# Moving the steps of a float64 weight conversion inside a matmul stage: new distances, split stores, later first loads

## The chip, the cores and the metric

The program runs on one core of a Trainium2 chip. The metric is the device time of one execution in microseconds (us), lower is better. The engines are named as in the profile: PE (matrix products), ACT (ScalarE), DVE (VectorE), POOL (GpSimd) and SP, which here issues every DMA, one after the other from one queue.

## The reference, cut to what matters

Three layers stand behind each other: a chunked state-space scan, a mixture of four experts over 3072 tokens, and a gated layer whose weights come in as float64.

```python
# x: scan output, (3072, 256)
for e in range(4):
    h = np.maximum(x @ w1[e], 0.0)                    # w1[e]: 256 x 1024
    out += p[:, e:e + 1] * (h @ w2[e])
...
g = x @ w_gate                                        # w_gate, w_val: 256 x 1536, float64
silu = g * (1.0 / (1.0 + np.exp(-g)))
val = x @ w_val
return (silu * val @ w_out).astype(np.float32)        # w_out: 1536 x 256, float64
```

## The kernel before, in words

Every product is formed three times, from a high and a low part of each operand (`high` rounds on ACT, L602; `low` subtracts the high part from the value, mostly on POOL, L605). The program has three stages.

First come the **units**: experts 0 and 1 on part of the tokens, mixed with the scan. Then come the **blocks**, the stage that the change is in: eight pairs (expert, pair of token blocks), `blocks` in the code, each cut in four **quads** (two 128-wide slices of the hidden layer). The text writes quad 3.1 for block 3, quad 1. Last come the **dense** quads of the float64 layer, 18 of them.

A quad of the block stage has four **parts** (0 to 3), the stretches between the `yield`s of `expert_hidden`. PE runs 45 matmuls of 512 columns in it: 21 for seven products (L829) and 24 that project the quad before (L928). Four accumulators X, Y, Z, W take the products, and other engines move them along:

- in part 0, ACT copies X into Y (L884), and PE may then add to Y;
- in part 1, ACT copies Y into Z (L887) and W aside (L889); in part 2 it copies Z aside (L892);
- in part 2, DVE adds that copy to W (L895) and the other to Y (L899). ACT rounds the four results (`hh`, L878) and DVE forms their low parts (`hl`, L879). The last `hl`, of key 12, is read from Z in part 3.

PE can't write X in the next quad before the `hl` of key 11 has read it, nor can ACT overwrite Y (L884 of the next quad) before the `hl` of key 21 has.

After each block, in quad 0 (parts 2 and 3) of the next one, DVE and POOL add the projected block to `acc` (L939, L940).

Between the parts stand side jobs. A table `todo` has a list of steps for each slot (block and quad, part), and they are emitted behind that part's own instructions, so each engine runs them in that order. The side jobs are

- `expert_quad`: the weights of the next expert. It loads a quad (L625, L626), rounds it on ACT, forms four sums on DVE (L612 to L615, 128x128 each, here called the expert sums) and low parts on POOL;
- `dense_tokens` and `expert_tokens`: sums and high and low parts of the tokens;
- `dense_quad`: the conversion of float64 weights, for g in 0..5 and for gate, val and out (0g, 0v, 0o, 1g, ... in the text). `load` fetches 512 KB as 32-bit words; `s0` (ACT, L678, L679) and `s1` (DVE, L683 to L685) build the float32 words, `s2` (DVE, L690) adds the last bit and, for gate and val, forms four sums on POOL; `s3` (ACT) and `s4` (POOL) form high and low parts of the first columns, `s5` and `s6` those of the sums, and `store` writes both to DRAM (L718, L721);
- `dense_load`: reads converted weights back (L733, L736), five DMAs for a dense quad. The first two, `dense_load(0, 0)` and `dense_load(0, 1)`, are side jobs of the block stage.

Tiles come from pools with rings of buffers. A tile that takes a used buffer waits until the last reader of the old tile is done, on the engine that writes the new one. `hh` and `hl` have five buffers each (`HB`), `f64` two, `dr` two, and the high and low tiles of the conversion (`wd_h`, `wd_l`) one each. `wd_o`, the tile of the output weights, takes the buffer of `wd_h`. Expert weights and re-read dense weights share 16 buffers (`wpool`).

The conversion's slots come from fixed offsets: with a the slot of the load, the steps of gate and val stand at a + 0, 3, 4, 5, 7, 8, 8, 9, 10, and the next conversion begins 6 slots later.

Of the kernel before, what the change touches and what calls it, by code (L numbers as in the profile page):

```python
# [23 lines left out]
def kernel(ctx: ExitStack, tc: tile.TileContext, nat_d, bc_d, bc0_d, a_d, probs, w1, w2, wg, wv, wo, out):  # L24
# [537 lines left out]
    def m_hidden(u):  # L562
        e, t, f = u
        o, n, vh, vl, _ = place(u)
        if f == FC1 // 2:
            pbc[e, t] = mpool.tile([P, 512], F32, tag="ma", name="pbc")[:, :n]
            nc.sync.dma_start(out=pbc[e, t], in_=probs_d[e:e + 1, o:o + n].to_broadcast([P, n]))
        ph = hidden_bank(n)
        hidden(ph, W1[e, f // NG], f % NG, vh, vl)
        hh = hpool.tile([P, 512], F32R, tag="hh", name="hh")[:, :n]  # L570
        hl = hpool.tile([P, 512], F32R, tag="hl", name="hl")[:, :n]
        nc.scalar.activation(out=hh, in_=ph, func=AF.Relu)  # L572
        nc.vector.scalar_tensor_tensor(out=hl, in0=ph, scalar=0.0, in1=hh.bitcast(F32), op0=ALU.max, op1=ALU.subtract)  # L573
        hid[u] = hh, hl
# [77 lines left out]

    HIGH = np_f32(0x0FEFFFFF)

    def dense_quad(g, what):

        V = nc.vector  # L660
        r = {}

        def load():
            f = r["f"] = raw_p.tile([P, 2, FQ, 2], I32, tag="raw", name="f64")
            if what == 2:
                src = wo[g * FQ:(g + 1) * FQ, :].rearrange("(k p) d -> p k d", p=P)
            else:
                src = (wg, wv)[what][:, g * FQ:(g + 1) * FQ].rearrange("(k p) f -> p k f", p=P)
            nc.sync.dma_start(out=f.rearrange("p k n w -> p k (n w)"), in_=src.bitcast(I32))
            f = f.rearrange("p k n w -> p (k n) w")  # L670
            r["hi"] = f[:, :, 1]
            r["lo"] = f[:, :, 0]
            r["byte"] = f.bitcast(U8)[:, :, 3]

        def s0():
            m = r["m"] = dpools["cv"].tile([P, 2 * FQ], I32, tag="wr", name="dr", bufs=2)
            m = m.bitcast(F32)
            nc.scalar.activation(out=m, in_=r["hi"].bitcast(F32), func=AF.Abs, scale=2.0**-112)  # L678
            nc.scalar.activation(out=r["lo"], in_=r["byte"], func=AF.Copy, scale=1 / 32, bias=1 / 64)  # L679

        def s1():
            m = r["m"].bitcast(F32)
            V.tensor_scalar(out=m, in0=m, scalar1=HIGH, scalar2=None, op0=ALU.min)  # L683
            V.tensor_scalar(out=r["m"], in0=r["m"], scalar1=3, scalar2=None, op0=ALU.logical_shift_left)
            V.scalar_tensor_tensor(  # L685
                out=r["m"], in0=r["hi"], scalar=-0x80000000, in1=r["m"], op0=ALU.bitwise_and, op1=ALU.bitwise_or
            )

        def s2():
            V.tensor_tensor(out=r["m"], in0=r["m"], in1=r["lo"], op=ALU.add)  # L690
            r["m"] = r["m"].bitcast(F32)
            if what < 2:
                r["s"] = r["f"].rearrange("p k n w -> p (k n w)").bitcast(F32)[:, :2 * FQ]
                gate_sums(r["m"], r["s"], nc.gpsimd)

        def s3():
            if what < 2:
                r["out"] = [dpools["cv"].tile([P, W7], F32R, tag=f"w{z}", name=f"wd_{z}") for z in "hl"]
                high(r["out"][0][:, RAW], r["m"][:, P:])
            else:  # L700
                r["out"] = [dpools["cv"].tile([P, 2, 2 * DM], F32R, tag="wh", name="wd_o")]
                high(r["out"][0][:, 0, :], r["m"])

        def s4():
            if what < 2:
                low(r["out"][1][:, RAW], r["m"][:, P:], r["out"][0][:, RAW])
            else:
                low(r["out"][0][:, 1, :], r["m"], r["out"][0][:, 0, :])

        def s5():  # L710
            high(r["out"][0][:, SUM], r["s"])

        def s6():
            low(r["out"][1][:, SUM], r["s"], r["out"][0][:, SUM])

        def store():
            if what == 2:
                nc.sync.dma_start(out=wo_d[g], in_=r["out"][0].bitcast(F32))  # L718
                return
            for z, v in enumerate(r["out"]):  # L720
# [144 lines left out]
    def expert_hidden(e, p, j):  # L865


        X, Y, Z, W = (bank(*b) for b in banks[:4])
        w = WE[e, j][0]
        V, S = nc.vector, nc.scalar  # L870
        part3, v = temp("c1"), temp("c1")
        add = lambda ps, a, x, start=False: product(ps, w, a, operand(p, x), start)

        def out(key, ps):
            hh = hpool.tile([P, 512], F32R, tag="hh", name="hh")
            hl = hpool.tile([P, 512], F32R, tag="hl", name="hl")
            hid[e, p, j, key] = hh, hl
            S.activation(out=hh, in_=ps, func=AF.Relu)  # L878
            return lambda: V.scalar_tensor_tensor(  # L879
                out=hl, in0=ps, scalar=0.0, in1=hh.bitcast(F32), op0=ALU.max, op1=ALU.subtract  # L880
            )

        add(X, A11, "B11", True)
        S.activation(out=Y, in_=X, func=AF.Copy)  # L884
        yield
        add(Y, S2, "T2")
        S.activation(out=Z, in_=Y, func=AF.Copy)  # L887
        add(W, S3, "T3", True)
# [58 lines left out]
    def dense_hidden(p, q, what, s):  # L947

        w = wq.pop((p, q, what))
        V = nc.vector  # L950

        def out(key, ps, add, dst):

            if what == 0:
                s[key] = temp("s")
                if add is not None:
                    V.tensor_tensor(out=s[key], in0=ps, in1=add, op=ALU.add)  # L957
                nc.scalar.activation(out=s[key], in_=ps if add is None else s[key], func=AF.Silu)  # L958
                return
            if add is not None:  # L960
                V.tensor_tensor(out=dst, in0=ps, in1=add, op=ALU.add)  # L961
            av = s.pop(key)
            V.tensor_tensor(out=av, in0=ps if add is None else dst, in1=av, op=ALU.mult)  # L963
            ah = hpool.tile([P, 512], F32R, tag="hh", name="ah")
            al = hpool.tile([P, 512], F32R, tag="hl", name="al")
            nc.scalar.activation(out=ah, in_=av, func=AF.Copy)  # L966
            low = V if (p, q) == quads[-1] and key in (12, 21) else nc.gpsimd
            low.tensor_tensor(out=al, in0=av, in1=ah.bitcast(F32), op=ALU.subtract)  # L968
            hid[p, q, key] = ah, al

        return seven(p, w, out)
# [33 lines left out]
    with tc.manual_schedule():  # L1005
        nc.sync.dma_start(out=la, in_=a_d)
        expert_load(0, 0)
        for q in range(NFIRST):
            a_load(q)
            a_load_nat(q)  # L1010
            Q[q]["L"] = [hpool.tile([P, 4, P], F32, tag=("hh", "hl")[q], name="L") for _ in range(2)]
        nc.sync.dma_start(out=pin, in_=probs)
        a_load(2)
        expert_load(0, 1)
# [54 lines left out]

        def job(steps, at):  # L1070
            for fn, a in zip(steps, at, strict=True):
                put(a + (a >= n0 and (a - n0) % 4 == 2 and fn.__name__ in ("s1", "s2", "sums")), fn)

        for j, a in enumerate((138, 146, 154, 161)):
            job(expert_quad(2, j), [a + o for o in (0, 4, 5, 7, 8, 9, 10)])
# [22 lines left out]
        a = quad(0, 1)  # L1098
        for g in range(NQD):
            for what in range(3):  # L1100
                while any((a + o - n0) % (4 * NQE) in (2, 3, 4) for o in (4, 5)):
                    a += 1
                job(dense_quad(g, what), [a + o for o in ((0, 3, 4, 5, 7, 8, 8, 9, 10) if what < 2 else (0, 3, 4, 5, 7, 8, 9))])
                a += 6 if what < 2 else 5
        assert a <= quad(7, 2)
        spread(dense_tokens(0), quad(6, 1), quad(7, 2))
        put(quad(6, 3, 2), lambda: dense_load(0, 0))
        put(quad(7, 1, 2), lambda: dense_load(0, 1))

        def at(*key):  # L1110
            for fn in todo.pop(key, []):
# [112 lines left out]
```

## Time and profile before

| what | value |
|---|---|
| time, median of 3 runs | 861.83 us (860.66 to 862.84) |
| the profiled execution, its own time | 863.37 us |
| its span, first to last instruction | 861.6 us |
| PE busy | 838.8 us (97%) |
| ACT, DVE, POOL busy | 462.3, 609.7, 442.7 us |
| mean granted clock of PE | 0.993 |

The profiled execution stands 1.54 us above the median of the runs. PE is idle for 22.8 us of the span; a busy PE can still be slow, since its matmuls overlap and its clock can be halved, so the length of a quad says more than its busy time.

### The profile page before, as it was taken

What the parts mean: (1) busy time and instruction counts of PE and PEld (TensorE: products, weight loads), DVE (VectorE), ACT (ScalarE), POOL (GpSimd) and SP (SyncE); (2) the same over time, 40 slices, a digit from 0 to 9 for tenths busy, and PEclk for the clock granted to TensorE, in tenths of its full rate; (3) what the DMA queues carried; (4) which work ended last, traced back from release to release, by engine and by line L of the source; (5) the groups of instructions that cost most, each with busy time, mean ns of one, the idle gap of its engine ahead of it and who ended that gap; (6) DMA issues with size and microseconds to landing.
All of it is one profiled execution on the core that took longest, in us unless ns stands there. A gap on an engine that the chain in (4) does not pass through costs nothing. (4 is left out here: it accounts for less than half of the span.)

```text
span 861.6 us, 12496 instructions
## 1 busy us (share of the span) xinstructions
PE 838.8 (97%) x4394; PEld 692.8 (80%) x4394; DVE 609.7 (71%) x895; ACT 462.3 (54%) x824; POOL 442.7 (51%) x389
## 2 busy tenths in 40 slices
PE   8899999999999999999999999899999999999998
PEld 7898778888878888878887878687888888888886
DVE  5987889767756756697977566547676667666665
ACT  6655555555476666667665566444444544434443
POOL 5865776445586622546664254307463664534251
PEclk9999999999999999999999999899999999999999
DMA  7854454435321235344532222653454274537301
GB/s 214 296 174 136 142 179 150 150 129 191 97 77 68 90 105 179 113 126 135 169 104 64 110 81 104 213 171 129 153 177 153 92 268 137 170 112 266 111 1 50
DMA packets 53623, 120.33 MB, mean 140 GB/s; under 512 B 5496, under 2 KB 19512, under 8 KB 53560
## 3 DMA queue, kind: packets, MB, share of 16 engines
q1 hardware_dynamic: 53560, 119.52, 41.4%
q8 instruction: 35, 0.57, 0.3%
q14 instruction: 28, 0.23, 0.1%
HBM read 102.06 MB, written 17.45 MB: 139 GB/s over the span
## 5 line engine op out<-in xcount | busy, mean ns | idle before, releaser
L968 POOL TENSOR_TENSOR al<-s,ah 128x512 fp32r<-128x512 f32 x70 | 103.4, 1507 | 126.0 <-issue 91.1
L966 ACT ACTIVATE ah<-s 128x512 fp32r<-128x512 f32 x72 | 45.3, 632 | 101.3 <-DVE s L963 85.4
L895 DVE TENSOR_TENSOR d<-d,c 128x512 f32<-128x512 f32 x32 | 22.3, 698 | 85.2 <-ACT c L892 85.1
L928 PE MATMUL d<-hh,we_o 128*128 128x512 f32 x256 | 79.8, 393 | 0.0
L928 PE MATMUL po<-hh,we_o 128*128 128x512 f32 x256 | 79.0, 390 | 0.5 <-DVE acc L594 0.5
L879 DVE SCALAR_TENSOR_TENSOR hl<-h,hh 128x512 fp32r<-128x512 f32 x96 | 66.1, 689 | 18.2 <-ACT hh L878 14.2
L572 ACT ACTIVATE hh<-h 128x512 fp32r<-128x512 f32 (+1 forms) x80 | 40.5, 510 | 67.5 <-PE h L531 67.5
L878 ACT ACTIVATE hh<-h 128x512 fp32r<-128x512 f32 x96 | 57.3, 597 | 27.9 <-DVE h L899 23.1
L573 DVE SCALAR_TENSOR_TENSOR hl<-h,hh 128x512 fp32r<-128x512 f32 (+1 forms) x80 | 45.9, 577 | 34.7 <-ACT hh L572 34.3
L845 DVE TENSOR_TENSOR u<-h,c 128x512 f32<-128x512 f32 x36 | 24.9, 690 | 56.8 <-PE h L829 37.9
L531 PE MATMUL h<-xh,w_h 128*128 128x512 f32 (+1 forms) x160 | 57.4, 359 | 4.3 <-DVE hl L573 3.4
L605 POOL TENSOR_TENSOR we_l<-raw_q,we_h 128x384 fp32r<-128x384 f32 (+1 forms) x32 | 37.8, 1180 | 45.0 <-ACT we_h L602 45.0
L539 PE MATMUL po<-hh,w_h 128*128 128x512 f32 (+1 forms) x160 | 57.4, 359 | 1.9 <-DVE acc L588 1.2
L829 PE MATMUL h<-xh,wq_h 128*128 128x512 f32 x144 | 56.8, 394 | 1.7 <-DVE v L847 1.1
L958 ACT ACTIVATE s<-s 128x512 f32<-128x512 f32 x54 | 33.4, 629 | 44.1 <-DVE s L957 43.4
L928 PEld LDWEIGHTS d<-hh,we_o 128*128 128x128 f32 x256 | 48.6, 190 | 10.3
L928 PEld LDWEIGHTS po<-hh,we_o 128*128 128x128 f32 x256 | 48.0, 188 | 10.9 <-ACT we_o L602 0.9
L531 PE MATMUL h<-xh,w_l 128*128 128x512 f32 (+1 forms) x160 | 56.1, 350 | 0.2 <-POOL w_l L143 0.2
L829 PE MATMUL h<-xh,wq_l 128*128 128x512 f32 x144 | 56.1, 390 | 0.0
L829 PE MATMUL h<-xl,wq_h 128*128 128x512 f32 x144 | 56.1, 389 | 0.0
L531 PE MATMUL h<-xl,w_h 128*128 128x512 f32 (+1 forms) x160 | 56.1, 350 | 0.0
L539 PE MATMUL po<-hh,w_l 128*128 128x512 f32 (+1 forms) x160 | 56.0, 350 | 0.0
(226 smaller groups left out, 2494.4 us busy)
## 6 DMA issues: line engine op xcount, KB each, us to landing
wq_h<-wd_d SPq DMA_DIRECT2D x36, 448.0 KB
wq_l<-wd_d SPq DMA_DIRECT2D x36, 448.0 KB
bc<-in_bc_dram SPq DMA_DIRECT2D x22, 512.0 KB
L<-crow_d SPq DMA_DIRECT2D x22, 512.0 KB
wq_o<-wo_d SPq DMA_DIRECT2D x18, 512.0 KB
raw_q<-in_w_dram SPq DMA_DIRECT2D x32, 256.0 KB
nat<-in_nat_dram SPq DMA_DIRECT2D x24, 256.0 KB
pbc<-probs_d SPq DMA_DIRECT2D x22, 256.0 KB
```

Of the source, the lines that this page charges most:

```text
L531: nc.tensor.matmul(ps, w[:, k, fs], v[:, k, :], start=(i == 0), stop=(i == len(ops) - 1))
L539: nc.tensor.matmul(po[d], w[:, fc, dsl], x, start=(first and i == 0), stop=(last and i == 2))
L572: nc.scalar.activation(out=hh, in_=ph, func=AF.Relu)
L573: nc.vector.scalar_tensor_tensor(out=hl, in0=ph, scalar=0.0, in1=hh.bitcast(F32), op0=ALU.max, op1=ALU.subtract)
L605: engine.tensor_tensor(out=out, in0=raw, in1=hi.bitcast(F32), op=ALU.subtract)
L829: nc.tensor.matmul(ps, x[:, ws], y, start=(start and i == 0), stop=(i == 2), skip_group_check=True)
L878: S.activation(out=hh, in_=ps, func=AF.Relu)
L879: return lambda: V.scalar_tensor_tensor(out=hl, in0=ps, scalar=0.0, in1=hh.bitcast(F32), op0=ALU.max, op1=ALU.subtract)
L928: nc.tensor.matmul(po[d], both[:, z, dsl], y, start=(first and i == 0), stop=(last and i == 2), skip_group_check=True)
L958: nc.scalar.activation(out=s[key], in_=ps if add is None else s[key], func=AF.Silu)
L966: nc.scalar.activation(out=ah, in_=av, func=AF.Copy)
L968: low.tensor_tensor(out=al, in0=av, in1=ah.bitcast(F32), op=ALU.subtract)
```

## The change

The conversion's steps get distances from the step before (`gap`) and a set of allowed parts of a quad: a step whose slot falls on another part moves on to the next that is allowed. `EARLY` is parts 0 and 1 (for `s0`), `SUMS` parts 0, 1 and 3, without part 3 of a block's quad 0 and part 0 of its quad 1 (for `s1` and `s2`), `CALM` parts 0 to 2 (for `s3` and `s5`). The store is split: the high part goes out one slot after `s5`, and the low part one slot after `s6`. `wd_o` gets a buffer of its own (`wo`). The ring of `hl` (with `al` and one use in the scan) gets four buffers where it had five. The first two dense loads move from quads 6.3 and 7.1 to quads 7.1 (part 3) and 7.3, and `dense_tokens(0)` begins two parts later.

```diff
-        hl = hpool.tile([P, 512], F32R, tag="hl", name="hl")[:, :n]
+        hl = hpool.tile([P, 512], F32R, tag="hl", name="hl", bufs=LAG + 1)[:, :n]
...
+    ANY, EARLY, SUMS, CALM = (0, 1, 2, 3), (0, 1), (0, 1, 3), (0, 1, 2)
...
-                r["out"] = [dpools["cv"].tile([P, 2, 2 * DM], F32R, tag="wh", name="wd_o")]
+                r["out"] = [dpools["cv"].tile([P, 2, 2 * DM], F32R, tag="wo", name="wd_o")]
...
-        def store():
-            if what == 2:
+        def store(z=None):
+            if z is None:
                 nc.sync.dma_start(out=wo_d[g], in_=r["out"][0].bitcast(F32))
-                return
-            for z, v in enumerate(r["out"]):
-                nc.sync.dma_start(out=wd_d[g, what, :, z, :], in_=v.bitcast(F32))
-
-        return [load, s0, s1, s2, s3, s4] + ([s5, s6] if what < 2 else []) + [store]
+            else:
+                nc.sync.dma_start(out=wd_d[g, what, :, z, :], in_=r["out"][z].bitcast(F32))
+
+        late = [(s5, 0, CALM), (lambda: store(0), 1, ANY), (s6, 0, ANY), (lambda: store(1), 1, ANY)]
+        return [(load, 0, ANY), (s0, 3, EARLY), (s1, 2, SUMS), (s2, 1, SUMS), (s3, 2, CALM), (s4, 1, ANY)] + (
+            late if what < 2 else [(store, 1, ANY)]
+        )
...
-                while any((a + o - n0) % (4 * NQE) in (2, 3, 4) for o in (4, 5)):
-                    a += 1
-                job(dense_quad(g, what), [a + o for o in ((0, 3, 4, 5, 7, 8, 8, 9, 10) if what < 2 else (0, 3, 4, 5, 7, 8, 9))])
-                a += 6 if what < 2 else 5
-        assert a <= quad(7, 2)
-        spread(dense_tokens(0), quad(6, 1), quad(7, 2))
-        put(quad(6, 3, 2), lambda: dense_load(0, 0))
-        put(quad(7, 1, 2), lambda: dense_load(0, 1))
+                at = a
+                for fn, gap, parts in dense_quad(g, what):
+                    at += gap
+                    while (at - n0) % 4 not in parts or parts is SUMS and (at - n0) % (4 * NQE) in (3, 4):
+                        at += 1
+                    put(at, fn)
+                a += 7 if what < 2 else 5
+        spread(dense_tokens(0), quad(6, 1, 3), quad(7, 2))
+        put(quad(7, 1, 3), lambda: dense_load(0, 0))
+        put(quad(7, 3), lambda: dense_load(0, 1))
```

The moved steps can be read in the order of three engines. Line numbers of the change are up to 5 higher for the same code.

**SP, from the load of 5v on (quad 6.3 before, quad 6.2 in the change).** `wq` is a dense load, `wd_d<-wd_h` and `wd_d<-wd_l` the stores of 5g and 5v, `f64` a load of the conversion, `pbc` the expert shares. Before:

```order
L669 DMA f64_5539<-in_wv_dram 128x2x512
L733 DMA wq_h_5593<-wd_d_102 128x896
L733 DMA wq_l_5594<-wd_d_102 128x896
L733 DMA wq_h_5597<-wd_d_102 128x896
L733 DMA wq_l_5598<-wd_d_102 128x896
L736 DMA wq_o_5601<-wo_d_103 128x1024
L721 DMA wd_d_102<-wd_h_5555 128x896
L721 DMA wd_d_102<-wd_l_5556 128x896
```

The same stretch in the change:

```order
L672 DMA f64_5498<-in_wv_dram 128x2x512
L721 DMA wo_d_103<-wd_o_5464 128x1024
L723 DMA wd_d_102<-wd_h_5587 128x896
L672 DMA f64_5650<-in_wo_dram 128x2x512
L723 DMA wd_d_102<-wd_l_5588 128x896
L950 DMA pbc_5749<-probs_d_100 128x512
L950 DMA pbc_5751<-probs_d_100 128x512
L723 DMA wd_d_102<-wd_h_5685 128x896
L723 DMA wd_d_102<-wd_l_5686 128x896
L738 DMA wq_h_5803<-wd_d_102 128x896
```

The five DMAs of the first dense load stood ahead of all the stores of 5g and 5v, and stand behind them now.

**DVE, quads 3.1 and 4.1, from the addition of the finished block to the sum of W.** `raw_q` has the expert sums, `dr` is `s1`. Quad 3.1 before:

```order
L939 TENSOR_TENSOR pbc_3791<-d2_3778,pbc_3791 128x512
L612 TENSOR_TENSOR raw_q_3990<-raw_q_3990 128x128
L613 TENSOR_TENSOR raw_q_3990<-raw_q_3990 128x128
L614 TENSOR_TENSOR raw_q_3990<-raw_q_3990 128x128
L615 TENSOR_TENSOR raw_q_3990<-raw_q_3990 128x128
L683 TENSOR_SCALAR dr_4173<-dr_4173 128x512
L684 TENSOR_SCALAR dr_4173<-dr_4173 128x512
L685 SCALAR_TENSOR_TENSOR dr_4173<-f64_4090,dr_4173 128x512
L895 TENSOR_TENSOR d0_4150<-d0_4150,c1_4152 128x512
```

In the change quad 3.1 has no `s1` at this place (its `s1` stands behind the quad's last `hl`), and quad 4.1, which had none, reads:

```order
L944 TENSOR_TENSOR pbc_4195<-d2_4182,pbc_4195 128x512
L612 TENSOR_TENSOR raw_q_4393<-raw_q_4393 128x128
L613 TENSOR_TENSOR raw_q_4393<-raw_q_4393 128x128
L614 TENSOR_TENSOR raw_q_4393<-raw_q_4393 128x128
L615 TENSOR_TENSOR raw_q_4393<-raw_q_4393 128x128
L686 TENSOR_SCALAR dr_4476<-dr_4476 128x512
L687 TENSOR_SCALAR dr_4476<-dr_4476 128x512
L688 SCALAR_TENSOR_TENSOR dr_4476<-f64_4398,dr_4476 128x512
L900 TENSOR_TENSOR d0_4558<-d0_4558,c1_4560 128x512
```

So the pattern of sums and `s1` ahead of W's addition leaves quad 3.1 and comes up in quad 4.1; quad 5.1 has it in both.

**ACT, from the rounding of key 21 in quad 6.3 to the copies of quad 7.0.** `dr` and `f64<-f64` are `s0` of 5v, `wd_h` is `s3` or `s5` of 5g, `t3h` and `xh1` are tokens. Before:

```order
L878 ACTIVATE hh_5578<-h1_5524 128x512
L602 ACTIVATE wd_h_5555<-f64_5414 128x512
L602 ACTIVATE t3h_0_98<-acc1_91 128x512
L602 ACTIVATE xh1_79<-acc1_91 128x512
L878 ACTIVATE hh_5607<-h2_5525 128x512
L678 ACTIVATE dr_5618<-f64_5539 128x512
L679 ACTIVATE f64_5539<-f64_5539 128x512
L884 ACTIVATE h1_5622<-h0_5621 128x512
L887 ACTIVATE h2_5623<-h1_5622 128x512
```

In the change:

```order
L883 ACTIVATE hh_5578<-h1_5519 128x512
L602 ACTIVATE wd_h_5587<-dr_5447 128x384
L883 ACTIVATE hh_5594<-h2_5520 128x512
L602 ACTIVATE t3h_0_98<-acc1_91 128x512
L602 ACTIVATE xh1_79<-acc1_91 128x512
L889 ACTIVATE h1_5613<-h0_5612 128x512
L602 ACTIVATE wd_h_5587<-f64_5336 128x512
L892 ACTIVATE h2_5614<-h1_5613 128x512
```

Five side instructions stood between the rounding of key 21 and the copy of X; now there are three, none of them `s0`.

## Rows read from the trace of the kernel before

**Rows 1.** Waits of PE (waited for: total us, times, longest):

```profile
PE h L829 <- ACT h L884: 6.0, 7, 3.1
```

**Rows 2.** Windows: stretch, length, busy time (count) of each engine, PEclk, DMA share, GB/s:

```profile
558.20:568.40 10.20, 10.20 (x47) 8.45 (x45) 6.10 (x11) 5.27 (x9) 1.29 (x1) 1.00 0.45 138
278.53:370.35 91.82, 91.82 (x406) 75.97 (x405) 63.05 (x102) 59.04 (x106) 37.76 (x40) 1.00 0.36 121
370.35:393.36 23.01, 21.00 (x92) 16.74 (x90) 19.09 (x29) 14.15 (x27) 14.47 (x15) 1.00 0.35 115
414.33:435.04 20.71, 20.70 (x91) 16.81 (x90) 18.42 (x29) 14.73 (x28) 15.44 (x16) 1.00 0.45 145
456.00:478.22 22.22, 21.06 (x91) 16.73 (x90) 16.76 (x25) 13.38 (x25) 11.70 (x12) 1.00 0.28 90
498.62:510.57 11.95, 10.50 (x46) 8.37 (x45) 9.82 (x15) 7.36 (x13) 7.77 (x5) 1.00 0.29 89
530.97:541.72 10.75, 10.50 (x46) 8.37 (x45) 7.80 (x12) 7.61 (x14) 5.74 (x7) 1.00 0.08 5
541.72:558.20 16.48, 13.35 (x47) 10.42 (x45) 7.41 (x12) 6.87 (x12) 7.14 (x5) 0.79 0.67 237
546.30:553.10 6.80, 6.05 (x14) 4.79 (x15) 0.00 (x0) 3.57 (x7) 5.03 (x4) 0.50 0.65 230
```

**Rows 3.** Timeline of SP around quads 6.3 to 7.1 (start, length):

```profile
516.69 0.61 SPq L733 DMA_DIRECT2D wq_l<-wd_d  x1
540.33 0.32 SPq L736 DMA_DIRECT2D wq_o<-wo_d  x1
540.75 0.38 SPq L721 DMA_DIRECT2D wd_d<-wd_h  x1
```

**Rows 4.** Timeline of ACT, same stretch (in brackets: idle before, and whom it waited for):

```profile
532.20 0.68 ACT L679 ACTIVATE f<-f 128x512 int32<-128x512 uint8 x1
532.76 0.61 ACT L884 ACTIVATE h<-h 128x512 f32<-128x512 f32 x1
...
545.99 0.52 ACT L602 ACTIVATE wd_h<-dr 128x384 fp32r<-128x384 f32 x1 [4.77 <-DMA wd_d<-wd_h]
546.42 0.58 ACT L884 ACTIVATE h<-h 128x512 f32<-128x512 f32 x1
```

**Rows 5.** Timeline of PE, quad 7.1:

```profile
547.05 0.80 PE L829 MATMUL h<-t24h,we_h 128*128 128x512 f32 x1 [3.13 <-ACT h L884]
```

**Rows 6.** Timeline of DVE, quad 3.1 (from 370.35):

```profile
373.96 0.28 DVE L612 TENSOR_TENSOR raw_q<-raw_q 128x128 f32<-128x128 f32 x1
374.27 1.29 DVE L613 TENSOR_TENSOR raw_q<-raw_q 128x128 f32<-128x128 f32 x1
...
378.07 1.24 DVE L683 TENSOR_SCALAR dr<-dr 128x512 f32<-128x512 f32 x1
...
380.41 0.69 DVE L895 TENSOR_TENSOR d<-d,c 128x512 f32<-128x512 f32 x1
```

**Rows 7.** Timeline of POOL, quad 3.1, its last operation in that run of work:

```profile
377.96 1.06 POOL L605 TENSOR_TENSOR we_l<-raw_q,we_h 128x384 fp32r<-128x384 f32 x1
```

**Rows 8.** Timeline of DVE, quad 4.1 (from 414.33):

```profile
422.11 0.68 DVE L895 TENSOR_TENSOR d<-d,c 128x512 f32<-128x512 f32 x1
```

**Rows 9.** Timeline of POOL, quad 4.1:

```profile
420.70 1.34 POOL L605 TENSOR_TENSOR we_o<-raw_q,we_o 128x512 fp32r<-128x512 f32 x1
```

**Rows 10.** Timeline of ACT, quad 6.1 (from 498.62):

```profile
503.82 0.63 ACT L602 ACTIVATE xh<-acc 128x512 fp32r<-128x512 f32 x1 [1.58 <-POOL acc L940]
504.36 0.58 ACT L887 ACTIVATE h<-h 128x512 f32<-128x512 f32 x1
```

**Rows 11.** Timeline of DVE, quad 7.2 (from 558.20), sum of W and the last two `hl`:

```profile
564.47 0.70 DVE L895 TENSOR_TENSOR d<-d,c 128x512 f32<-128x512 f32 x1 [3.80 <-ACT c L892]
...
567.17 1.45 DVE L879 SCALAR_TENSOR_TENSOR hl<-h,hh 128x512 fp32r<-128x512 f32 x2
```

**Rows 12.** Timeline of ACT, quad 7.3 (from 568.40):

```profile
571.32 0.58 ACT L887 ACTIVATE h<-h 128x512 f32<-128x512 f32 x1 [1.46 <-PE h L829]
```

More of the change, by code (lines that the diff above doesn't have):

```diff
@@ L875, in out @@
             hh = hpool.tile([P, 512], F32R, tag="hh", name="hh")
-            hl = hpool.tile([P, 512], F32R, tag="hl", name="hl")
+            hl = hpool.tile([P, 512], F32R, tag="hl", name="hl", bufs=LAG + 1)
             hid[e, p, j, key] = hh, hl
@@ L964, in out @@
             ah = hpool.tile([P, 512], F32R, tag="hh", name="ah")
-            al = hpool.tile([P, 512], F32R, tag="hl", name="al")
+            al = hpool.tile([P, 512], F32R, tag="hl", name="al", bufs=LAG + 1)
             nc.scalar.activation(out=ah, in_=av, func=AF.Copy)
@@ L1010 @@
             a_load_nat(q)
-            Q[q]["L"] = [hpool.tile([P, 4, P], F32, tag=("hh", "hl")[q], name="L") for _ in range(2)]
+            Q[q]["L"] = [hpool.tile([P, 4, P], F32, tag=("hh", "hl")[q], name="L", bufs=(HB, LAG + 1)[q]) for _ in range(2)]
         nc.sync.dma_start(out=pin, in_=probs)
@@ L1071, in job @@
             for fn, a in zip(steps, at, strict=True):
-                put(a + (a >= n0 and (a - n0) % 4 == 2 and fn.__name__ in ("s1", "s2", "sums")), fn)
+                put(a + (a >= n0 and (a - n0) % 4 == 2 and fn.__name__ == "sums"), fn)
         for j, a in enumerate((138, 146, 154, 161)):
```

## The prediction

> **What bounds the kernel now.** The table has PE busy for 97% of the span, so I first asked what a quad of the block stage takes when nothing holds it, and then which quads take longer. The windows answer both. Quad 7.2 takes 10.20 us, and the nine quads from 1.0 to 3.0 take 91.82 together, which is 9 x 10.20 [rows 2]. That is 45 matmuls at 0.227 us, PE's pace at full clock. Every us that a quad takes beyond 10.20 is therefore a stall, and a step that moves inside that cover is worth nothing.
>
> The other windows show the stalls [rows 2]: quads 3.1 and 3.2 together 23.01 - 20.40 = 2.61; quad 7.0 10.75 - 10.20 = 0.55 (three such: 4.0, 4.3 and 7.0); 4.1 and 4.2 together 0.31; 5.1 and 5.2 together 1.82; 6.1 1.75; 7.1 6.28. The sum is 2.61 + 3 x 0.55 + 0.31 + 1.82 + 1.75 + 6.28 = 14.42 us. The waits of PE say through whom most of it comes: the copy of X into Y on ACT, 6.0 us in 7 waits, one of 3.1 [rows 1]. The timelines then tell what stood ahead of that copy in each place.
>
> **Quad 7.1 (6.28 us): a store behind a blocked queue.** SP issued a dense load at 516.69 and its next DMA, the output weights' load, at 540.33: nearly 24 us, two quads and more. The store of 5g's high part, next in line, left at 540.75 [rows 3]. ACT's `s3` of 5v needs that tile, waited 4.77 us for the store and ran at 545.99, and the copy of X behind it ran at 546.42 [rows 4]. PE stood for 3.13 us [rows 5], and then its granted clock was 0.50 for 6.80 us (1.2 GHz instead of 2.4) [rows 2]; half of those 6.80 us, 3.4, is lost work, and 3.13 + 3.4 is about the 6.28.
> In the change the dense load stands behind both stores of 5v, so the output weights' tile, which needs a buffer that an expert's weights hold, keeps no store back. The store of 5g's high part now stands one slot behind `s5`, and `s3` of 5v one slot after that. That is short, so I checked the times: `s5` runs before the copy of Y, which starts 2.92 into a clean quad (571.32 - 568.40) [rows 12], and a store took 5.2 us from issue to the start of the instruction that it held (540.75 to 545.99) [rows 3, 4]. It lands 8.2 into quad 7.0 at the latest; `s3` stands behind the rounding of key 21, whose low part starts at 567.17 - 558.20 = 8.97 [rows 11]. So `s3` doesn't wait, if SP is free. I take the whole 6.28 as removed.
> The first dense quad begins two quads (20.4 us) after 7.1. If its five DMAs (2.3 MB) are issued at the end of 7.1 and move at the 237 GB/s of the busiest window [rows 2], they need 10 us. The next five are issued in 7.3 and are wanted a dense quad (66 matmuls, 15 us) after the first begins. I cost both at nothing; a load that came late would cost its lateness, one for one.
>
> **`s0` at the end of a quad (3 x 0.55).** In 6.3 `s0` stands between part 3's rounding and the copy of X in 7.0. Its second instruction starts at 532.20 and the copy at 532.76, 1.79 after quad 7.0 began (530.97) [rows 4, 2]; in a clean quad the copy would start 0.88 after (571.32 less a product and a projection, 9 matmuls or 2.04, less 568.40) [rows 12]. `EARLY` puts every `s0` into parts 0 and 1, where it has 2.04 us between the two copies and the wait of PE behind them. Removed: 1.65. The work that stays in parts 2 and 3 (two roundings of expert weights and one of the conversion, or three of tokens in 6.1) is three instructions where five made 0.55 of stall; two fewer, 0.56 apart [rows 4], take 1.1 off, so I cost it at nothing.
>
> **Token step in 6.1 (1.75).** The copy of Y started at 504.36, 5.74 into the quad, behind a rounding of tokens that waited for POOL's addition to `acc` and ran at 503.82 [rows 10]. That addition belongs to quad 6.0's last parts and is done 5.2 into 6.1. The step now stands in part 3, after 8 us, and finds its input there. Removed: 1.75.
>
> **`s1` behind the expert sums (3.1 before, 4.1 in the change, 5.1 in both).** After a block, DVE adds three pieces to `acc`, then the expert sums run: 0.28 for the first and 1.29 for the second, though they have one shape; the four took 378.07 - 373.96 = 4.11 in 3.1 while POOL worked [rows 6]. `s1` came next, 2.34 us (378.07 to 380.41), and W's sum started 10.06 into the quad instead of 6.27 [rows 6, 11]: 3.79 late, for 2.61 us of stall. Quad 4.1 had the sums without `s1`: W's sum started at 422.11 - 414.33 = 7.78, 1.51 late, for 0.31 [rows 8, 2]. So a delay costs about itself less 1.2.
> - In 3.1 `s1` goes behind the last `hl`, and the quad becomes what 4.1 was: 2.61 - 0.31 = 2.30 removed.
> - In 4.1 `s1` comes in. The bounds: 5.1, which has the same pattern, cost 1.82 [rows 2]; at the upper end, POOL works longer here. Its run ended at 377.96 + 1.06 = 379.02 in 3.1 [rows 7], just as the first instruction of `s1` ended; in 4.1 it has one 128x512 low part more (`s4` of 2o), 1.34 by its neighbour [rows 9], so the other two may be slowed too and `s1` may take 2.34 + 1.3 = 3.6, which gives 1.51 + 3.6 - 1.2 = 3.9. I take 3.0, between them and nearer 3.1's 2.61. Added: 3.0 - 0.31 = 2.7.
> - In 5.1 only the owner of `s1` changes (3o for 4g): nothing.
>
> The Trainium skill (SBUF — State Buffer, section Who interferes with whom) has the ports that DVE and POOL share as an exclusive lock: a DVE instruction with two SBUF inputs or in a two-port mode waits for the whole POOL instruction. The 1.29 beside 0.28 [rows 6] agrees. By that rule all three instructions of `s1` in 4.1 would wait for a POOL instruction each, which is the second rival.
>
> **The rings.** With four `hl` buffers the low part of key 12 can't start before PE has projected the same key of the quad before, which ends with the quad. In 7.2 it started 0.76 after 567.17, at 567.93 [rows 11], and the quad ended at 568.40: the wait is 0.5 us. Z, which it reads, is overwritten by the copy of Y at 571.32 [rows 12], 2.2 us after the delayed low part is done, and DVE's next fixed task is W's sum, 6.27 into the quad. Cost: nothing. If that cover were gone, see the third rival. The loads of the conversion now often wait on SP until the conversion before has freed its buffer, and loads of expert weights queue behind them; `s0` then has a part less of reserve in 2.3, and DVE has `s1`, sums and `s2` between quads 2.3 and 3.0. Neither shows in the trace of before. Lower bound nothing, upper bound one small stall of each kind (0.56 + 0.56); I take 0.4.
>
> **The sum.** Removed 6.28 + 1.65 + 1.75 + 2.30 = 12.0; added 2.7 + 0.4 = 3.1; net 8.9. The profiled execution took 863.37 and would take 854.5. It stood 1.54 above the median of the runs, 861.83, from which the same 8.9 give **852.9**.
>
> **Rivals.**
> 1. *The sums meet no stall.* If `s1` in 4.1 and 5.1 falls into pauses of POOL, the 2.7 is nearer 0 and part of 5.1's 1.82 goes too: 848.5 to 850.5. Against it: the sums took over 4 us there each time. 0.12.
> 2. *DVE is held longer.* If each of the three instructions of `s1` in 4.1 waits for one of POOL (1.34 [rows 9]), `s1` takes 4.0, the stall 1.51 + 4.0 - 1.2 = 4.3 and the sum 1.3 more: 854.2. The same in 2.3, 3.0 and 4.2, where `s1` stands just ahead of sums, adds up to as much in each: 854.5 to 858.5 together. For it: 4.1's POOL run is the longest. 0.16.
> 3. *Slower: the ring of four.* If the low part of key 12 were held past the next quad's copy of Y, more than 2.2 us beyond what I worked out, each of 31 quads would end late by the wait of 0.5: 15 us, 868. Against it: PE's order puts that projection at the quad's end, not later. 0.05.
> 4. *The stall at the end isn't gone.* `s3` of 5v still waits for the store, if SP is held at that moment by a DMA that waits for POOL; the margin is 0.7 us. PE would stand and its clock fall again, up to 6.28 back: 859.2, no change that can be told. 0.07.
>
> **How the numbers follow.** The forecast (850.5 to 854.5) has 0.60, and the rivals the rest. The range 848.5 to 858.5 takes in the forecast and the first two and leaves out the last two. 0.3% (2.6 us) is about what a measurement of this kernel can tell from no change: faster than 859.2 are the forecast, rivals 1 and 2, 0.88; rival 4 is the same, 0.07; rival 3 is slower, 0.05.
>
> **What would show it.** Right: quads 7.0 and 7.1 at 10.2, no fall of the granted clock between them, no gap of SP over some 10 us ahead of the last stores; 4.3, 6.1 and 4.0 at 10.2; 3.1 and 3.2 together about 20.7; 4.1 and 4.2 together about 23.4. Wrong: a wait of PE over 1 us in another quad of blocks 2 to 4 (ACT behind a load, or DVE behind `s1`), a wait for dense weights at the start of the dense stage, or a last `hl` that holds the copy of Y.

## The result, and the profile after the change

The changed kernel takes 855.04 us (median of 4 runs, 854.79 to 855.87) and the kernel before 862.34 (4 runs): a ratio of 0.9916, 95% interval 0.9893 to 0.9939. It is 7.3 us faster; 8.9 were predicted, 852.9 us, in a range of 848.5 to 858.5. The profiled execution has a span of 853.2 us (861.6 before). The 852.9 was counted from 861.83, the median of before at that time; with its fourth run that median is 862.34, so 0.5 of the 2.1 us between forecast and result lies in the base.

From the first matmul of quad 0.0 to that of the first dense quad the changed kernel takes 333.53 us, the kernel before 340.72. So 7.19 us were saved in the block stage. The units ahead of it took 1.12 less, which is inside their spread: over the 13 traces of this study their length goes from 236.0 to 238.8 us. The dense stage behind it took 282.92 us (283.05 before), so the two later dense loads cost nothing there, as the prediction had it.

The waits of PE on the copy of X have shrunk from 6.0 us to 1.8, as [rows 1] show it for before; a wait for DVE is new (waited for: total us, times, longest):

```profile
PE h L834 <- DVE hl L884: 2.2, 2, 2.0
...
PE h L834 <- ACT h L889: 1.8, 3, 1.0
```

The windows after (columns as in [rows 2]) are those of quad 3.0; 3.1 and 3.2 together; 4.1 and 4.2; a piece of 4.2; 5.1 and 5.2; and, behind the cut, 7.0 and 7.1:

```profile
359.37:370.57 11.20, 10.48 (x46) 8.37 (x45) 9.56 (x17) 7.90 (x16) 6.69 (x8) 1.00 0.45 142
370.57:391.21 20.64, 20.64 (x92) 16.74 (x90) 18.72 (x30) 14.19 (x28) 14.32 (x15) 1.00 0.47 147
411.61:435.91 24.30, 22.28 (x92) 17.98 (x90) 20.13 (x29) 14.10 (x27) 14.66 (x15) 0.93 0.33 108
423.94:427.36 3.42, 3.37 (x8) 2.70 (x9) 2.45 (x4) 2.76 (x7) 1.28 (x1) 0.50 0.97 315
456.31:478.50 22.19, 21.01 (x92) 16.74 (x91) 19.72 (x29) 12.56 (x23) 11.50 (x12) 1.00 0.21 72
...
529.49:549.89 20.40, 20.40 (x91) 16.90 (x90) 15.11 (x22) 13.64 (x25) 14.40 (x14) 1.00 0.44 145
```

Set against 10.20 a quad they give the stalls, in us (single quads by their first matmuls):

| quads | before | predicted | after |
|---|---|---|---|
| 7.1 | 6.28 | 0 | 0 |
| 4.0, 4.3, 7.0 | 1.65 | 0 | 0 |
| 6.1 | 1.75 | 0 | 0.01 |
| 3.1 + 3.2 | 2.61 | 0.31 | 0.24 |
| 4.1 + 4.2 | 0.31 | 3.0 | 3.90 |
| 5.1 + 5.2 | 1.82 | 1.82 | 1.79 |
| 1.2, 2.3, 3.0 (small delays) | 0.02 | 0.4 | 1.37 |

The removed part came as forecast. Both added terms were larger: 4.1 by 0.9 and the small delays by 1.0.

**What happens at 7.0 and 7.1.** SP and ACT after (start, length; in brackets the idle time before and its releaser):

```profile
531.52 0.32 SPq L723 DMA_DIRECT2D wd_d<-wd_h  x1
...
547.01 0.32 SPq L723 DMA_DIRECT2D wd_d<-wd_l  x1
547.38 0.47 SPq L738 DMA_DIRECT2D wq_h<-wd_d  x1
```

```profile
538.33 0.52 ACT L602 ACTIVATE wd_h<-dr 128x384 fp32r<-128x384 f32 x1
```

The store of 5g's high part leaves at 531.52, `s3` of 5v runs at 538.33 without a wait, and the dense load comes behind all four stores. Before, the same store left at 540.75 and `s3` waited 4.77 us [rows 3, 4]. SP still issues nothing for 14.4 us ahead of that store (its DMA before is at 516.83). But here the store waits for its own data: `s5` of 5g ends at 531.49, and both quads take 10.20.

**What happens in 4.1.** DVE (from the second of the expert sums, the next two cut), POOL and PE after:

```profile
415.53 1.29 DVE L613 TENSOR_TENSOR raw_q<-raw_q 128x128 f32<-128x128 f32 x1
...
419.34 1.51 DVE L686 TENSOR_SCALAR dr<-dr 128x512 f32<-128x512 f32 x1
420.88 1.12 DVE L687 TENSOR_SCALAR dr<-dr 128x512 int32<-128x512 int32 x1
422.04 0.69 DVE L688 SCALAR_TENSOR_TENSOR dr<-f,dr 128x512 int32<-128x512 int32 x1
422.65 0.69 DVE L900 TENSOR_TENSOR d<-d,c 128x512 f32<-128x512 f32 x1
```

```profile
419.23 1.34 POOL L605 TENSOR_TENSOR we_o<-raw_q,we_o 128x512 fp32r<-128x512 f32 x1
420.53 1.19 POOL L605 TENSOR_TENSOR we_l<-raw_q,we_h 128x384 fp32r<-128x384 f32 x1
```

```profile
423.99 0.79 PE L834 MATMUL h<-xh,we_h 128*128 128x512 f32 x1 [2.02 <-DVE hl L884]
```

`s1` held DVE from 419.34 to 422.65, 3.31 us, against 2.34 in the old place [rows 6]. Its first two instructions each end just after a POOL instruction (420.57, 421.72); the third finds POOL idle and takes 0.69. W's sum starts 11.04 us into the quad and PE stands for 2.02 us.

**What happens in 3.0.** ACT after, from quad 2.3:

```profile
355.43 0.68 ACT L681 ACTIVATE dr<-f 128x512 f32<-128x512 f32 x1 [2.15 <-DMA f<-in_wg_dram]
...
361.63 0.60 ACT L889 ACTIVATE h<-h 128x512 f32<-128x512 f32 x1
```

`s0` of 2g waits 2.15 us for its load, and the rest of ACT's work in 2.3 comes behind it. The rounding of key 21 starts 0.27 us before the quad ends (359.10, of 359.37) where run 9, with `s0` out of the way, has 1.49; so the copy of X of 3.0 starts 2.26 into the quad where a clean one has 0.88.

**What happens in 1.1.** Here `s1` ran beside POOL in both kernels. Its third instruction after:

```profile
293.12 2.77 DVE L688 SCALAR_TENSOR_TENSOR dr<-f,dr 128x512 int32<-128x512 int32 x1
```

It took 1.67 before, and 0.69 in 4.1, where POOL was idle. A low part of 2.57 us, started at 292.76, ran on POOL beside it. W's sum starts 8.19 into the quad (7.08 before), and quad 1.2 loses 0.21. That the one makes the other is a reading of the trace; no run tests it.

### The profile page after: what moved, and what is told of

Same layout as the page of the kernel before. It is cut to its first block, busy times and chain, and to the rows that moved or that the text cites. A ratio compares the mean times of both kernels' runs of the same rounds, so it can differ in the third digit from the quotient of the medians.

```text
span 853.2 us, 12526 instructions
## 1 busy us (share of the span) xinstructions
PE 837.3 (98%) x4394; PEld 693.4 (81%) x4394; DVE 615.7 (72%) x895; ACT 460.7 (54%) x824; POOL 445.9 (52%) x389
## 4 chain that ended last, share of the span: by engine, by line
PE 84%; DVE 7%; ACT 2%; issue 2%; DMA 2%; POOL 1%; SPq 0%; DVEq 0%; POOLq 0%; ACTq 0%
PE h L834 27%; PE po L539 10%; PE h L531 9%; PE d L933 8%; PE po L933 8%; PE d L834 8%; PE d L997 6%; PE po L997 5%; PE scores L410 1%; PE ypsum L456 1%; PE ypsum L419 1%; DVE hl L884 1%; DVE d L900 1%; DMA f<-in_wg_dram 1%; DMA L<-crow_d 0%
## 5 line engine op out<-in xcount | busy, mean ns | idle before, releaser
L883 ACT ACTIVATE hh<-h 128x512 fp32r<-128x512 f32 x96 | 57.2, 597 | 26.6 <-DVE h L904 22.8
L377 POOL TENSOR_TENSOR Bs<-bc,Bs 64x512 fp32r<-64x512 f32 x22 | 34.7, 1575 | 41.7 <-issue 23.9
```

## Experiments

Ratios are to the kernel before, run on the same chip; line numbers are those of the changed kernel, and quads are counted as above.

**1. The first dense loads alone put back** (changed kernel).

```diff
-        put(quad(7, 1, 3), lambda: dense_load(0, 0))
-        put(quad(7, 3), lambda: dense_load(0, 1))
+        put(quad(6, 3, 2), lambda: dense_load(0, 0))
+        put(quad(7, 1, 2), lambda: dense_load(0, 1))
```

> The changed kernel with the first two dense loads alone put back to quads 6.3 and 7.1. My theory (a dense load that waits for a buffer of the expert weights holds SP, and the store of 5g's high part stands behind it): SP is held until about 1.4 us before quad 7.1, the store is late, `s3` of 5v waits some 5 us on ACT, PE stands about 3 to 4 us and its granted clock falls to 0.50 as it did before the change: quad 7.1 takes 5 to 7 us more than 10.2, and the kernel 860 to 862. Rival (the split stores and the new distances cure it by themselves, the place of the loads is idle): within 1 us of the changed kernel's 855.0.

Measured: 861.91 us, ratio 1.0003 (0.9992 to 1.0015). The whole gain is gone. Window of quad 7.1, then SP and ACT:

```profile
540.12:557.06 16.94, 12.10 (x46) 9.52 (x45) 7.01 (x11) 8.28 (x15) 8.38 (x6) 0.90 0.66 224
```

```profile
519.45 0.42 SPq L738 DMA_DIRECT2D wq_l<-wd_d  x1
538.73 0.32 SPq L741 DMA_DIRECT2D wq_o<-wo_d  x1
539.15 0.38 SPq L723 DMA_DIRECT2D wd_d<-wd_h  x1
```

```profile
544.58 0.52 ACT L602 ACTIVATE wd_h<-dr 128x384 fp32r<-128x384 f32 x1 [5.72 <-DMA wd_d<-wd_h]
```

Quad 7.1 takes 16.94 us. One DMA that waits for its buffer stands on SP for 19 us, and `s3` waits for the store behind it. The Trainium skill (DMA: Bandwidth & Descriptors, section Anatomy of one DMA — SWDGE (gpsimd) path) has a DMA's wait made by the engine that issues it, and not by the DMA engines; the section is about DMAs that POOL issues. These rows of SP agree: it issues nothing from 519.87 to 538.73, and then the waiting DMAs one after the other.

**2. The loads alone moved later** (kernel before): `quad(6, 3, 2)` and `quad(7, 1, 2)` become `quad(7, 1, 3)` and `quad(7, 3)`.

> The kernel before with nothing but the first two dense loads moved to quads 7.1 (part 3) and 7.3. My theory: the 6.28 us of quad 7.1 go, quad 7.1 takes 10.2 to 10.5 with the granted clock at 1.0, and the kernel about 856.0 (862.3 less 6.3); the other stalls (3.1, 4.0, 4.3, 5.1, 6.1, 7.0) stay as they were. Rival (both stores of a conversion, one behind the other at the old place, still hold `s3`): quad 7.1 keeps 2 us or more, and the kernel takes 858 or more.

Measured: 856.84 us, ratio 0.9948 (0.9934 to 0.9962). Window of quad 7.1 (7.0 keeps its stall):

```profile
542.60:552.80 10.20, 10.20 (x46) 8.45 (x45) 7.39 (x12) 6.41 (x11) 7.18 (x5) 1.00 0.31 97
```

In the profiled execution the block stage is 6.28 us shorter (334.44 for 340.72), as the theory has it; the medians differ by 4.4, less than the 6.3 expected. The stall that goes isn't of one size: quad 7.1 lost 6.28 in the trace of before, 5.07 in that of run 4 and 6.74 in that of run 1, since its clock was low for 6.8, 3.4 and 3.4 us and PE stood for 3.1, 3.4 and 4.8.

**3. `s1` of 3g and 3o behind the last `hl`, the later steps with it** (changed kernel).

```diff
-                    while (at - n0) % 4 not in parts or parts is SUMS and (at - n0) % (4 * NQE) in (3, 4):
+                    while (at - n0) % 4 not in parts or parts is SUMS and ((at - n0) % (4 * NQE) in (3, 4) or at in (quad(4, 1, 1), quad(5, 1, 1))):
```

> The changed kernel, with `s1` of 3g in block 4 and of 3o in block 5 put into part 3 of quads 4.1 and 5.1, behind the quad's last `hl` (where the change itself has it in 3.1), and the later steps of these two conversions moved with it. My theory (`s1` behind the expert sums makes W's sum late): quads 4.1 and 4.2 fall from 3.9 us over 20.4 to about 0.3, quads 5.1 and 5.2 from 1.8 to about 0.3, the granted clock doesn't fall in 4.2, and the kernel takes about 850 (855.0 less 5.1). Rival (DVE has the same work to do either way and W's sum of 4.2 and 5.2 is late instead, or the sums beside POOL's long run are the cause): the stalls only move one quad on, and the kernel takes 853.5 to 855.5.

Measured: 860.31 us, ratio 0.9988 (0.9977 to 1.0000): neither. Windows of 4.1, of 5.0, and of 5.1 with 5.2:

```profile
412.78:422.98 10.20, 10.20 (x46) 8.45 (x45) 10.06 (x14) 5.27 (x10) 7.47 (x6) 1.00 0.17 53
...
444.83:464.13 19.30, 12.90 (x46) 10.13 (x45) 8.67 (x12) 8.35 (x16) 5.63 (x5) 0.82 0.51 177
464.13:484.82 20.69, 20.69 (x91) 16.81 (x90) 19.31 (x29) 11.71 (x22) 9.49 (x10) 1.00 0.16 52
```

The stalls behind the sums went as expected (4.1 to 0, 5.1 and 5.2 to 0.29), but 4.2 kept 1.45, and 9.1 us came up in 5.0. SP and ACT show why:

```profile
424.27 0.73 SPq L626 DMA_DIRECT2D raw_q<-in_w_dram  x1
444.64 0.37 SPq L672 DMA_DIRECT2D f<-in_wo_dram  x1
...
446.08 0.46 SPq L723 DMA_DIRECT2D wd_d<-wd_h  x1
```

```profile
451.88 0.52 ACT L602 ACTIVATE wd_h<-dr 128x384 fp32r<-128x384 f32 x1 [7.27 <-DMA wd_d<-wd_h]
```

It is the stall of 7.1 once more, in another place: SP issues nothing for 20 us, since the load of 3o waits for a buffer that `s6` of 3g frees, and `s6` had moved with the rest; the store of 3g's high part stands behind that load, and `s3` of 3v waits for the store.

The same trace separates DVE's own speed from POOL's work. In quad 4.2 POOL was idle from 426.2 to 429.62, and DVE ran there:

```profile
426.55 0.43 DVE L687 TENSOR_SCALAR dr<-dr 128x512 int32<-128x512 int32 x1
...
427.94 0.29 DVE L613 TENSOR_TENSOR raw_q<-raw_q 128x128 f32<-128x128 f32 x1
```

They take 0.43 us where 4.1 had 1.12, and 0.29 where it had 1.29. So the length of the sums, and of the first two instructions of `s1`, is mostly POOL's.

**4. The ring of four alone** (kernel before): `bufs=LAG + 1` for `hl`, `al` and the use in the scan, as in the change.

> The kernel before with nothing but the ring of the low parts (`hl`, `al` and the use in the scan) at four buffers instead of five. My theory: the low part of key 12 starts up to 0.7 us later in a quad and nothing waits for it; within 1 us of the kernel before (862.3). Rival (the delayed low part holds the copy of Y): about 0.5 us in each of 31 quads, up to 15 us, 870 or more.

Measured: 861.86 us, ratio 1.0001 (0.9990 to 1.0013). No cost.

**5. `s1` alone behind the last `hl`** (changed kernel).

```diff
-                    put(at, fn)
+                    put(at + {(3, 0, "s1"): 2, (3, 2, "s1"): 2}.get((g, what, fn.__name__), 0), fn)
```

> As the run before with `s1` of 3g and 3o behind the last `hl` of quads 4.1 and 5.1, but with no other step of these conversions moved. After that run I have two theories for its 9.1 us in quad 5.0. First: its own cause is that the later steps moved too (SP issued a load of 3o that waits for `s6` of 3g, now a part later, and the stores of 3g stood behind it); then without that shift 5.0 takes 10.2, quads 4.1 and 5.1/5.2 are at 0 and 0.3 as they were there, 4.2 keeps about 1.5 (a rounding on ACT that waits for its load, issued behind the store of 2o), and the kernel takes 0.5% less than the changed kernel, a ratio to the kernel before of about 0.987. Rival: `s1` in part 3 is itself what delays the chain behind it, and 5.0 or a quad near it keeps a stall of several us: a ratio of 0.992 or more.

Measured: 851.33 us, ratio 0.9874 (0.9858 to 0.9890). Windows of 4.2, 5.0, and 5.1 with 5.2:

```profile
423.10:434.37 11.27, 10.77 (x46) 8.29 (x45) 8.37 (x16) 8.84 (x18) 7.00 (x9) 1.00 0.59 185
444.57:454.77 10.20, 10.20 (x46) 8.45 (x45) 8.47 (x12) 8.00 (x16) 5.25 (x5) 1.00 0.28 106
454.77:475.44 20.67, 20.67 (x92) 16.82 (x90) 19.22 (x29) 11.95 (x22) 10.29 (x11) 1.00 0.21 70
```

The first theory holds: 5.0 is clean, 4.1 takes 10.20 as in run 3, and 5.1 with 5.2 are at 0.27. What is left in 4.2 is 1.07, where ACT waits for a load of expert weights:

```profile
426.60 0.53 ACT L602 ACTIVATE we_h<-raw_q 128x384 fp32r<-128x384 f32 x1 [1.38 <-DMA raw_q<-in_w_dram]
```

**6. Two more steps moved**: to run 5 is added `s0` of 2g one part later, and the store of 2o two parts later.

```diff
-                    put(at, fn)
+                    put(at + {(3, 0, "s1"): 2, (3, 2, "s1"): 2, (2, 0, "s0"): 1, (2, 2, "store"): 2}.get((g, what, fn.__name__), 0), fn)
```

> As the run with `s1` alone, and two further single steps moved: `s0` of 2g one part later (2.3, part 2), where the trace of the change has it waiting 2.1 us for its load, and the store of 2o two parts later (4.1, part 2), behind the load of expert weights that it kept back. My theory: quads 2.3 and 3.0 lose most of their 1.2 us, and 4.2 its 1.5: a ratio of about 0.984 to the kernel before. Rival: `s0` in part 2 is in the way of the copy of Z there and costs 0.5 or more, and the load of the expert weights is late for another reason: the ratio stays at 0.987.

Measured: 849.58 us, ratio 0.9856 (0.9841 to 0.9871), between the two. Window of 4.2:

```profile
421.05:431.51 10.46, 10.46 (x46) 8.37 (x45) 8.37 (x15) 8.81 (x18) 6.94 (x9) 1.00 0.15 49
```

Quad 4.2 fell to 0.27: the store of 2o had kept the load back (it left at 420.59 in run 5, and the load behind it at 421.50; here the load is out at 409.68). Quad 5.2 rose by 0.28, to 0.55; why stays open. Quad 3.0 kept 0.88. ACT, from quad 2.3:

```profile
359.01 0.62 ACT L602 ACTIVATE wd_o<-dr 128x512 fp32r<-128x512 f32 x1
359.53 0.65 ACT L681 ACTIVATE dr<-f 128x512 f32<-128x512 f32 x1
360.08 0.66 ACT L682 ACTIVATE f<-f 128x512 int32<-128x512 uint8 x1
360.62 0.60 ACT L883 ACTIVATE hh<-h 128x512 fp32r<-128x512 f32 x1
361.10 0.61 ACT L889 ACTIVATE h<-h 128x512 f32<-128x512 f32 x1
```

No wait is left there, only five side instructions between key 21's rounding and the copy of X: the three shown ahead of key 12's rounding (L883), and two roundings of expert weights ahead of them. That half of my theory fell.

**7. The token step of 6.1 back in part 0** (changed kernel): `spread(dense_tokens(0), quad(6, 1), quad(7, 2))`.

> The changed kernel with the token step of quad 6.1 alone back at its old place (part 0). My theory: the copy of Y in 6.1 waits behind a rounding that waits for POOL's addition to `acc`; quad 6.1 takes 1.75 us more than 10.2, the kernel 0.2% more than the changed one (a ratio of about 0.9935 to the kernel before). Rival: the addition comes earlier in the changed kernel, as POOL has other work there; quad 6.1 stays at 10.2, a ratio of 0.9915.

Measured: 857.12 us, ratio 0.9946 (0.9931 to 0.9961). Windows of 4.1 with 4.2, and of 6.1:

```profile
411.33:435.32 23.99, 21.00 (x91) 16.74 (x90) 20.13 (x29) 14.00 (x27) 14.63 (x15) 1.00 0.35 109
498.32:510.26 11.94, 10.49 (x47) 8.37 (x45) 10.02 (x14) 6.78 (x12) 9.47 (x7) 1.00 0.11 29
```

Quad 6.1 loses 1.74, as forecast. Quads 4.1 and 4.2 have the code of the changed kernel, and here no fall of the clock: 3.59 instead of 3.90.

**8. Three `s0` back in part 3** (changed kernel): of 3g in 3.3, of 3o in 4.3, of 5v in 6.3.

> The changed kernel with three `s0` back in part 3 and nothing else moved: 3g (quad 3.3, one part earlier), 3o (quad 4.3, one part earlier) and 5v (quad 6.3, two parts later). My theory: each delays the copy of X of the next quad, 0.55 us in each of 4.0, 5.0 and 7.0, together 1.65 and a ratio of about 0.9935 to the kernel before; the copy of X starts 1.8 after the quad's start. Rival: what made 0.55 was the number of roundings beside it, and with fewer of them in part 3 nothing shows: 0.9915.

Measured: 856.06 us, ratio 0.9931 (0.9916 to 0.9946), which settles nothing by itself. The windows of 4.0 and 5.0 do (that of 7.0 reads as that of 5.0):

```profile
400.52:410.75 10.23, 10.23 (x47) 8.39 (x46) 9.27 (x16) 7.14 (x14) 3.02 (x3) 1.00 0.16 52
444.92:455.56 10.64, 10.49 (x47) 8.38 (x45) 8.46 (x12) 8.09 (x16) 5.23 (x5) 1.00 0.37 122
```

They lose 0.03, 0.44 and 0.44, 0.91 together, where the theory had 1.65. Only 4.0 and 7.0 are places of before; 5.0 had no stall there, and 4.3 isn't tested. So part of it is the rival's: ahead of the copy of X in 4.0 stand four side instructions instead of five, which is all but free; 5.0 and 7.0 have five.

**9. `s0` of 2g behind the copy of X of 3.0** (run 6 with `(2, 0, "s0"): 3` and `(2, 0, "s1"): 1`).

> As the run with three moves, but `s0` of 2g stands behind the copy of X of quad 3.0 (part 0 there, with its `s1` right behind it) instead of in part 2 of 2.3, where it still left 0.88 us in 3.0. My theory: what costs in 3.0 is five side instructions between the rounding of key 21 in 2.3 and the copy of X in 3.0; with three of them 3.0 falls to 0.3 or less, and the kernel to a ratio of about 0.985 to the kernel before (0.6 us under the run with three moves). Rival: `s1` then starts about 3 us into 3.0 and stands with the expert sums and `s2` ahead of W's sum, which comes after 6.3; 3.0 or 3.1 keeps 0.6 or more, the stall only changes its place.

Measured: 850.21 us, ratio 0.9858 (0.9842 to 0.9874). Window of 3.0:

```profile
359.96:370.16 10.20, 10.20 (x46) 8.45 (x45) 8.67 (x15) 7.64 (x16) 6.30 (x8) 1.00 0.47 157
```

Quad 3.0 is clean (3.1 and 3.2 have 0.29 between them), and the block stage is down to 327.57 us, from 328.16 in run 6. A gain of 0.6 us is too little for the times to show: runs 6 and 9 are equal, both about 1.4% faster than the kernel before and 0.6% faster than the changed one by their ratios.

**10 and 11. Pauses of PE made longer** (run 5 with the later store of 2o; `s0` of 0v, 1g, 1o, 4v, 5g and 5o in part 3). The numbers are those of run 10; run 11 has 3, 4, 5, 3, 4 and 5.

```diff
-            nc.scalar.activation(out=m, in_=r["hi"].bitcast(F32), func=AF.Abs, scale=2.0**-112)
+            for _ in range(1 + {(0, 1): 2, (1, 0): 3, (1, 2): 4, (4, 1): 5, (5, 0): 6, (5, 2): 7}.get((g, what), 0)):
+                nc.scalar.activation(out=m, in_=r["hi"].bitcast(F32), func=AF.Abs, scale=2.0**-112)
...
```

> The run with `s1` alone and the later store of 2o, with `s0` of six conversions put into part 3 of a quad without expert weights on ACT, and their first instruction repeated 2, 3, 4, 5, 6 and 7 times more (quads 0.3, 1.2, 2.1, 5.2, 6.1, 7.0; it writes the same values again). Each repetition should lengthen PE's wait for the copy of X in the next quad by 0.56 us: idle times of about 1.3, 1.8, 2.4, 2.9, 3.5 and 4.1. Theory one (the length of PE's pause decides): the granted clock stays at 1.0 behind the short ones, and is 0.50 behind those from some length between 1.5 and 3.1 on, so that these quads cost more than their pause. Rival (a fall is rare and by chance): it falls behind one or two of any length.

> As the run ahead of it, with 3, 4, 5, 3, 4 and 5 repetitions more in the same six places (idle times of about 1.8, 2.4 and 2.9, each twice). Theory one: pauses of one length are followed by the same granted clock. Rival: pauses of one length are followed by a fall in one place and by none in the other.

Measured, one run each: 882.01 and 879.32 us. Quad 1.3 of run 10, and PE's pauses in its quads 1.3 and 2.2:

```profile
310.02:323.92 13.90, 12.12 (x46) 9.54 (x45) 3.97 (x6) 8.00 (x14) 1.89 (x2) 0.88 0.63 217
```

```profile
314.00 0.50 PE L835 MATMUL h<-t24h,we_h 128*128 128x512 f32 x1 [1.78 <-ACT h L890]
```

```profile
348.56 0.79 PE L835 MATMUL h<-t24h,we_h 128*128 128x512 f32 x1 [2.04 <-ACT h L890]
```

Quads 1.3 and 5.3 of run 11, and the pauses in them:

```profile
311.75:324.73 12.98, 10.50 (x47) 8.37 (x46) 3.95 (x6) 8.67 (x15) 1.88 (x2) 1.00 0.68 232
485.57:498.20 12.63, 10.51 (x46) 8.37 (x45) 4.39 (x7) 8.89 (x16) 2.73 (x3) 1.00 0.42 156
```

```profile
316.43 0.50 PE L835 MATMUL h<-t24h,we_h 128*128 128x512 f32 x1 [2.48 <-ACT h L890]
```

```profile
489.89 0.50 PE L835 MATMUL h<-t24h,we_h 128*128 128x512 f32 x1 [2.12 <-ACT h L890]
```

Pauses of 1.78 and 2.04 us were followed by a clock of 0.50 (a mean of 0.88 in both quads), pauses of 2.12 and 2.48 were not (1.00 in both), and the quad with 1.78 cost more (13.90) than the one with 2.48 (12.98). Theory one falls for these lengths; the rival in its strict form (one or two falls, behind a pause of any length) falls too, since each pause of the block stage from 2.9 us on, in all traces here, was followed by a fall. In quads 5.3 to 7.1 the pauses of run 10 became 3.5 to 7.0 us, longer than I had worked out, and I didn't follow up why.

## Why the prediction was right, and where it was off

- **7.1 (6.28, shown).** The blocked queue was the whole cause: the loads alone bring it back (run 1) and take it away (run 2). The split of the stores and the tile of its own for the output weights weren't needed for it: run 2 has neither. The 6.28 is the size in one trace, though: others have 5.07 and 6.74, and run 2's medians give 4.4.
- **Token step (1.75, shown).** 1.74 in run 7.
- **`s0` in part 3 (1.65, right in sum, cause shown in part).** All three places are clean after the change. Of the two that run 8 tests, `s0` alone brings back 0.44 of 0.55 in 7.0 and 0.03 in 4.0; 4.3 wasn't tested. The step's reason, five side instructions against three, holds better than its wording: in run 8 a fourth is nearly free, a fifth costs 0.44.
- **3.1 (2.30, right).** 2.37 went. No run puts this `s1` back alone; run 5 makes the same move in 4.1 and 5.1, with the same outcome.
- **The rings (0, shown).** Run 4; rival 3 is out.
- **4.1 (added 2.7, mis-sized; 3.90 - 0.31 = 3.59).** The step that failed is "I take 3.0, between them". The formula of that very step (1.51 late, plus the length of `s1`, less 1.2) gives a stall of 3.6 with the measured 3.31, and run 7 shows 3.59 for the pair of quads; the other 0.31 of the 3.90 came with the fall of the clock after the pause of 2.02. So it is chance that the 3.90 equals the upper bound. The old 2.61 of 3.1 was the wrong neighbour, since POOL had one low part less there. Rival 2 has the mechanism (each instruction of `s1` waits for one of POOL) and was right for two of three: POOL's run was over when the third began. Beside POOL, in 1.1, that third instruction took 2.77 where it takes 0.69 alone. The Trainium skill (SBUF — State Buffer, section Who interferes with whom) has a DVE instruction with two inputs in SBUF contend with one of POOL that reads SBUF. The rule agrees with 0.69 and 2.77, and with the sums' 0.29 and 1.29.
- **Small delays (0.4, mis-sized; 1.37).** I named the mechanism, `s0` a part short of reserve in 2.3, and bounded it by "one small stall of each kind". But 3.0 had 1.01: a wait of 2.15 us for the load reached ACT's work for the next quad. Run 9 shows that with `s0` out of the way the 1.01 goes entirely; run 6, that without the wait, but with five instructions there, 0.88 stays. The rest is 0.15 in 2.3 and 0.21 in 1.2, a place that the prediction didn't name.
- **Their sum.** Removed 12.0 as forecast; added 4.9 instead of 3.1 (3.59, and 1.37 less the 0.02 of before), which leaves 7.1 of the 8.9, and the block stage lost 7.19.
- **Its signs.** Those of being right held in 7.0 and 7.1, in 4.0, 4.3 and 6.1, and in 3.1 and 3.2 (20.64 for about 20.7). One of being wrong came true: PE waited 2.02 us for DVE behind `s1` in 4.1, and 4.1 with 4.2 took 24.30 for about 23.4. The range was wide enough for it.

## What to carry to other kernels

Where one queue issues every DMA, ask of each one what it waits for and what stands behind it: a load placed ahead of a store may hold it for 20 us, which run 3 made happen again by moving steps that looked free. In this kernel a step was best put right behind the instruction that the critical engine waits for, and moved alone: two `s1` moved by two parts were worth 0.4% (run 5), and the same two with their followers cost 0.7%. Price elementwise work by a row that had the same neighbour engine at work, not by the nearest row of its kind.

## What the runs showed of the hardware that I had not expected

- A pause of PE of 2.02 us in quad 4.1 was followed by 3.42 us at 0.50 in the changed kernel, by a fall of the same length in run 1, and by none in runs 7 and 8, which have the same code in that quad and pauses of 2.02 and 2.01; 1.78 and 2.04 were followed by a fall where 2.12 and 2.48 weren't. So the length of a pause alone doesn't decide it. The Trainium skill (TensorE: Matmul & The Clock Gate, section What's actually happening) has the clock's check running free of the program. By that the same pause can meet it or miss it, which fits; no run here shows the check itself.
- A fall need not cost half its length. In 4.2 it cost 0.31 us (3.90 less 3.59), because PE waits there anyway (0.97 us for the copy of X, in the trace of run 7; in that of the changed kernel no such wait is left); in quad 1.3 of run 10, with no wait behind it, the quad with the shorter pause by 0.70 us (1.78 for 2.48) took 0.92 more than the quad of run 11, so the fall cost 1.62.
- POOL's work stretches a DVE sum of 128x128 from 0.29 to 1.29 us, a 128x512 shift from 0.43 to 1.12, and the third instruction of `s1` from 0.69 to 2.77.
